# Weight refills of a routed expert layer: four parts in four slots, and an early product moved past the refill tables

## The chip, the cores and the metric

The kernel runs on one core of a Trainium2 chip. The metric is the device time of one execution in microseconds (us); before the change the median of 3 runs is 1395.26 us (1395.2 to 1396.17). The engines are TensorE (PE in the rows; PEld is its weight load), VectorE (DVE), ScalarE (ACT), GpSimd (POOL) and SyncE (SP), which here issues nearly all transfers.

## The reference

Three layers in a row on 4608 tokens of width 512: attention within chunks of 64 (8 heads), a dense layer of width 2048, and a routed layer with 8 experts of width 1024. Only the last matters here:

```python
expert_idx = np.argmax(x @ w_gate, axis=1)
for e in range(E):
    mask = expert_idx == e
    h = np.maximum(x[mask] @ w1[e], 0.0)
    out[mask] = gate_w[mask, None] * (h @ w2[e])
```

Each token goes through one expert, and how many go to which is known only once all of them have been gated.

## The kernel before

**Slots.** While the dense layer runs, each token's row is written to a table in DRAM (`xs`), sorted by expert. The expert stage then works through it in slots: one slot is a block of 128 tokens of one expert. Blocks of one expert stand next to each other. A static loop (line 948) covers `TS` = 39 slots, numbered from 0; an optional tail covers more.

**Weights.** An expert's weights are four parts of 2 MB: parts 0 and 1 are the two halves of `w1`, parts 2 and 3 those of `w2`. They lie split in two float32r pieces in DRAM (`wsp`), and in `ring[0]` to `ring[3]` on chip. Every ring tile has two halves, so that one expert can be in work while the next one's part is loaded. Which half a slot reads is a run-time value (`rt` row 0, read by TensorE's sequencer in `m1`, line 683).

**What a slot does.** `load(t)` (line 637): SP reads the slot's place and issues five transfers, the input rows in four and two columns (`gi`) in a fifth; the input has three buffers. `tx(t)` transposes the input (VectorE) and splits it (ScalarE, GpSimd). `m1(t, 0)` and `m1(t, 1)` are 12 products of 128x512 each, with parts 0 and 1; evictions go to ScalarE for the first and to VectorE for the second. `th(t, f)` transposes and splits the result. `m2(t, 0)` and `m2(t, 1)` are 12 products each with parts 2 and 3; then the result is scaled and scattered to the output. All products are recorded on line 677.

**Refills.** `refill(t, c)` (line 856) is called for every slot t from 4 on and every part c, and issues one transfer from SP (line 861) with a condition that is read from `rt[3 + c, t]`. Where the condition is 0, nothing is moved, but SP goes through the instruction and its waits all the same. The transfer writes the half that slot t doesn't read. Since halves are run-time values, the bookkeeping sees a write of the whole part; line 869 declares that the readers in slots t and t+1 don't depend on it, so the first products that wait for `refill(t, c)` are those of slot t+2 with part c. In the other direction the refill waits for the last product of slot t-1 with that part.

**Order.** The order of work is written by hand: every engine runs its instructions in the order of the program. Up to slot 5 it is the list `START` (line 886). From then on the loop's iteration t records tx(t+2), m1(t+1, 0), refill(t, 0), m1(t+1, 1), refill(t, 1), th(t+1), m2(t, 0), refill(t-1, 2), m2(t, 1), refill(t-1, 3), load(t+4). So on SP four refills and one load follow each other in each iteration, in order.

**Tables.** The rows of `rt` are made on VectorE on one partition, for 50 slots at once. `table_refill` (line 840) makes the conditions: `mt` is the number of blocks of the slot's expert less 2, `rr` the place of the slot in its expert (0, 1, ...), `has` says that there is a next expert to load. The expert of the first slots needs no refill: the first two experts are loaded ahead. Before the change part c is loaded in the slot in which `rr` is min(mt, c // 2), that is parts 0 and 1 in the expert's first slot and parts 2 and 3 in its second (all four in the first where it has two blocks).

Of the kernel before, what the change touches and what calls it, by code (L numbers as in the profile page):

```python
# [12 lines left out]
ALU = mybir.AluOpType  # L13
# [29 lines left out]
def tile_attention_moe(ctx, tc, q, k, v, w_in, w_out, alpha, w_gate, w1, w2, out):  # L43
# [13 lines left out]
    T = NTILE + 2 * (E - 1)  # L57
# [525 lines left out]
    V = nc.vector  # L583
# [133 lines left out]
    def tbl(shape, name, dt=F32):  # L717
        tb[name] = P2["tb"].tile(shape, dt, name=name)
        return tb[name]

    def bc(x, a, b, p=128):
        return x.unsqueeze(1).to_broadcast([p, b - a, E])
# [90 lines left out]
    def slot_sum(dst, vals):  # L813
        w = tb["w"][o1]
        V.tensor_tensor(out=w, in0=tb["oh"][o1], in1=vals, op=ALU.mult)
        V.tensor_reduce(out=dst, in_=w, axis=AX.X, op=ALU.add)
# [23 lines left out]
    def table_refill():  # L840
        q_ = tb["ordt"]
        mt, rr, cm, has = (tbl([1, T], x) for x in ("mt", "rr", "cm", "has"))
        mo = tbl([1, 1], "mo")
        V.tensor_reduce(out=mo, in_=tb["pos8"][o1, 1], axis=AX.X, op=ALU.max)
        V.tensor_scalar(out=has, in0=q_, scalar1=mo[:, 0:1], scalar2=None, op0=ALU.is_lt)
        V.scalar_tensor_tensor(out=has, in0=q_, scalar=0.5, in1=has, op0=ALU.is_gt, op1=ALU.mult)
        V.scalar_tensor_tensor(out=has, in0=tio[o1], scalar=tb["S"][o1, 0:1], in1=has, op0=ALU.is_lt, op1=ALU.mult)
        slot_sum(mt, bc(tb["m"][o1], 0, T, 1))
        slot_sum(rr, tb["d"][o1])
        V.tensor_copy(out=rt[:, 7, T:T + 1], in_=tb["S"][o1])  # L850
        V.tensor_scalar(out=mt, in0=mt, scalar1=-2.0, scalar2=None, op0=ALU.add)
        for c in range(4):
            V.scalar_tensor_tensor(out=cm, in0=mt, scalar=float(c // 2), in1=rr, op0=ALU.min, op1=ALU.is_equal)
            V.tensor_tensor(out=rt[:, 3 + c, 0:T], in0=cm, in1=has, op=ALU.mult)

    def refill(t, c):
# [23 lines left out]
    for t in range(3):  # L880
# [11 lines left out]
        (load_early, 1, 3), (table_own, 0, 8), (table_base, 0, 8), (th, 2, 0), (table_own, 8, T), (th, 2, 1), (load, 4),  # L892
        (tx, 4), (m1, 3, 0), (table_order,), (m2, 1, 0), (m1, 3, 1), (m2, 1, 1), (load, 5), (m2, 2, 0), (th, 3, 0),
        (tx, 5), (m2, 2, 1), (table_next,), (load, 6), (th, 3, 1), (m1, 4, 0), (m1, 4, 1), (tx, 6), (th, 4, 0),
        (table_base, 8, T), (m2, 3, 0), (th, 4, 1), (load, 7), (table_refill,), (m1, 5, 0), (refill, 4, 0), (load, 8),
        (m2, 3, 1), (th, 5, 0), (m1, 5, 1), (refill, 4, 1), (m2, 4, 0), (th, 5, 1), (m2, 4, 1),
    )
    FIRST = 5

# [123 lines left out]
```

## Time and profile before

| what | before |
|---|---|
| median of 3 runs | 1395.26 us |
| the profiled execution, its own time | 1394.91 us |
| its span, first to last instruction | 1393.1 us |
| PE busy | 1333.0 us (96%) |
| PEld busy | 1153.9 us (83%) |
| DVE busy | 1028.5 us (74%) |
| ACT busy | 817.2 us (59%) |
| POOL busy | 744.2 us (53%) |
| granted TensorE clock, mean | 0.99 |

The page of the profile cuts the span into 40 slices and gives each engine's busy share in tenths; PE stands at 9 from the fifth slice to the 37th, with one 8. The share says little about single waits: a few us in a slice of 35 don't show. They are found in the view of waits (who waited for whom) and in the timeline, which has one line for a run of like instructions on an engine: start, duration, engine, line, operation, names, count, and in brackets the idle time before it and what ended it. A line that begins with `SPq` is an issue by SyncE; its duration is that of the issue, not of the transfer. The expert stage runs from 933 us to the end.

### The profile page before, as it was taken

What the parts mean: (1) busy time and instruction counts of PE and PEld (TensorE: products, weight loads), DVE (VectorE), ACT (ScalarE), POOL (GpSimd) and SP (SyncE); (2) the same over time, 40 slices, a digit from 0 to 9 for tenths busy, and PEclk for the clock granted to TensorE, in tenths of its full rate; (3) what the DMA queues carried; (4) which work ended last, traced back from release to release, by engine and by line L of the source; (5) the groups of instructions that cost most, each with busy time, mean ns of one, the idle gap of its engine ahead of it and who ended that gap; (6) DMA issues with size and microseconds to landing.
All of it is one profiled execution on the core that took longest, in us unless ns stands there. A gap on an engine that the chain in (4) does not pass through costs nothing. (4 is left out here: it accounts for less than half of the span.)

```text
span 1393.1 us, 31133 instructions
## 1 busy us (share of the span) xinstructions
PE 1333.0 (96%) x9515; PEld 1153.9 (83%) x9515; DVE 1028.5 (74%) x2526; ACT 817.2 (59%) x2281; POOL 744.2 (53%) x754
## 2 busy tenths in 40 slices
PE   7788999999999999999999999999899999989997
PEld 6667888998999999999999998887688888868775
DVE  7996688788788878878887886668966655555553
ACT  4554565656656565656656564349565566646554
POOL 4553457666665766666666664334444444424443
PEclk9999999999999999999999999999999999999999
DMA  6545445556556665655566551293124416865543
GB/s 231 197 151 183 146 161 199 187 189 207 197 171 200 196 204 182 202 183 194 179 216 197 168 184 45 62 413 112 43 61 167 167 54 224 340 243 209 173 167 147
DMA packets 107306, 249.16 MB, mean 179 GB/s; under 512 B 15552, under 2 KB 36544, under 8 KB 103040
## 3 DMA queue, kind: packets, MB, share of 16 engines
q1 hardware_dynamic: 101136, 227.37, 48.1%
q0 software_dynamic: 6000, 19.70, 3.7%
q8 instruction: 84, 1.38, 0.4%
q14 instruction: 86, 0.70, 0.2%
HBM read 401.39 MB, written 88.91 MB: 352 GB/s over the span
## 5 line engine op out<-in xcount | busy, mean ns | idle before, releaser
L328 PEld LDWEIGHTS h<-xt,ring 128*128 128x128 f32 x3456 | 455.8, 192 | 41.7 <-DVE xt L315 4.0
L328 PE MATMUL h<-xt,ring 128*128 128x256 f32 x3456 | 465.8, 285 | 14.3 <-DVE xt L315 3.5
L380 PE MATMUL y<-ring,g 128*128 128x512 f32 x1728 | 457.5, 400 | 5.4 <-POOL g L358 3.0
L380 PEld LDWEIGHTS y<-ring,g 128*128 128x128 f32 x1728 | 307.5, 190 | 62.9 <-POOL g L358 4.7
L358 POOL TENSOR_TENSOR g<-r,g 128x256 fp32r<-128x256 f32 x281 | 249.3, 890 | 137.3 <-ACT g L354 121.4
L404 DVE CUSTOM_DVE_ANT_0 junk<-row,wgb 128x512 bf16<-128x512 f32 x288 | 267.5, 929 | 7.8 <-ACT row L392 3.6
L468 POOL TENSOR_TENSOR sp<-eraw,sp 128x512 fp32r<-128x512 f32 x128 | 181.8, 1421 | 132.4 <-ACT sp L467 117.0
L695 DVE TENSOR_SCALAR hx<-h 32x128 f32<-32x128 f32 x576 | 165.3, 287 | 108.5 <-PE h L677 101.1
L677 PE MATMUL h<-ring,xT 128*128 (+1 forms) x936 | 227.7, 398 | 11.3 <-DMA ring<-wsp 9.9
L665 POOL TENSOR_TENSOR hT<-z,hT 128x512 fp32r<-128x512 f32 x78 | 100.6, 1308 | 238.5 <-ACT hT L664 238.5
L677 PE MATMUL y<-ring,hT 128*128 (+1 forms) x936 | 221.5, 391 | 5.0 <-POOL hT L665 3.0
L677 PEld LDWEIGHTS h<-ring,xT 128*128 128x128 f32 x936 | 176.5, 189 | 55.2 <-issue 6.7
L677 PEld LDWEIGHTS y<-ring,hT 128*128 128x128 f32 x936 | 175.2, 188 | 45.5 <-POOL hT L665 4.7
L354 ACT ACTIVATE g<-r 128x256 fp32r<-128x256 f32 x288 | 119.5, 415 | 151.7 <-DVE r L350 109.6
L344 ACT ACTIVATE r<-h 128x256 f32<-128x256 f32 x288 | 109.9, 381 | 159.5 <-POOL g L358 74.5
L693 ACT ACTIVATE hx<-h 32x128 f32<-32x128 f32 x672 | 179.6, 267 | 12.7 <-PE h L677 5.2
L664 ACT ACTIVATE hT<-z 128x512 fp32r<-128x512 f32 x78 | 48.0, 632 | 131.4 <-DVE z L662 127.2
L257 ACT ACTIVATE px<-s 32x256 f32<-32x256 f32 x240 | 89.7, 374 | 3.8 <-DVE s L246 0.9
L467 ACT ACTIVATE sp<-eraw 128x512 fp32r<-128x512 f32 x128 | 81.1, 633 | 1.0
L662 DVE STREAM_TRANSPOSE z<-xg 128x512 f32<-128x512 f32 x39 | 27.6, 708 | 47.3 <-POOL hT L665 47.2
L665 POOL TENSOR_TENSOR xT<-z,xT 128x512 fp32r<-128x512 f32 x39 | 52.2, 1337 | 16.7 <-ACT xT L664 16.2
L269 POOL TENSOR_TENSOR px<-px,sr 128x512 f32<-128x512 f32 x30 | 34.1, 1136 | 39.8 <-DVE sr L268 39.8
(734 smaller groups left out, 1192.9 us busy)
## 6 DMA issues: line engine op xcount, KB each, us to landing
ring<-wsp SPq DMA_DIRECT2D x148, 2048.0 KB
wsp<-sp SPq DMA_DIRECT2D x128, 512.0 KB
eraw<-in_w SPq DMA_DIRECT2D x128, 256.0 KB
xg<-xs SPq DMA_DIRECT2D x156, 64.0 KB
vt<-in_v SPq DMA_DIRECT2D x18, 512.0 KB
qt<-in_q SPq DMA_DIRECT2D x17, 512.0 KB
kt<-in_k SPq DMA_DIRECT2D x17, 512.0 KB
iraw<-in_w_in SPq DMA_DIRECT2D x16, 512.0 KB
```

The source lines that it names most:

```text
L257: nc.scalar.activation(out=p[J:J + 32, t], in_=s[I:I + 32, e], func=ACTF.Exp, scale=scale)
L328: nc.tensor.matmul(out=h, lhsT=w[:, wl, a, 128 * mi:128 * mi + 128], rhs=x[:, xl, a], start=(n == 0), stop=(n == 11),)
L344: nc.scalar.activation(out=r, in_=h, func=ACTF.Relu)
L354: nc.scalar.activation(out=gs[j, m][:, 0], in_=rs[j, m][0], func=ACTF.Copy)
L358: eng.tensor_tensor(out=g[:, 1], in0=r, in1=g[:, 0].bitcast(F32), op=ALU.subtract)
L380: nc.tensor.matmul(out=ys[j][t], lhsT=g[:, gl, 128 * t:128 * t + 128], rhs=w[:, wl, mi], start=(m == 0 and n == 0), stop=(m == MF - 1 and ...
L404: nc.vector.tensor_tensor_reduce(out=junk, in0=r[:, 0:512], in1=wgb[e // 2][:, e % 2], scale=1.0, scalar=0.0, op0=ALU.mult, op1=ALU.add, a ...
L468: eng.tensor_tensor(out=dst[:, 1], in0=raw, in1=dst[:, 0].bitcast(F32), op=ALU.subtract)
L665: nc.gpsimd.tensor_tensor(out=dst[:, 1], in0=z, in1=dst[:, 0].bitcast(F32), op=ALU.subtract)
L677: ins.append(nc.tensor.matmul(out=out, lhsT=lhs[:, xl, a], rhs=w[:, rows_, wl, a], start=(first and a == 0 and n == 0), stop=(last and a = ...
L693: nc.scalar.activation(out=dst, in_=src, func=ACTF.Relu)
L695: V.tensor_scalar(out=dst, in0=src, scalar1=0.0, scalar2=None, op0=ALU.max)
```

## The change

Two edits. In `table_refill`, parts 1 and 2 get their own condition: with `far` = 1 where the slot's expert has five or more blocks (`mt` >= 3) and 0 elsewhere, part 1 is loaded where `rr` is min(mt, 0) + far, part 2 where it is min(mt, 1) + far; part 0 where it is min(mt, 0) as before, and part 3 where it is min(mt, 3). So an expert with five or more blocks loads parts 0, 1, 2 and 3 of the next in its slots 0, 1, 2 and 3; one with four blocks in 0, 0, 1 and 2; one with three in 0, 0, 1, 1 and one with two in its first slot, both as before. In `START`, `m1(5, 0)` moves in front of `table_refill`, and `load(8)` moves from behind `refill(4, 0)` to behind `refill(4, 1)`.

```diff
         V.tensor_scalar(out=mt, in0=mt, scalar1=-2.0, scalar2=None, op0=ALU.add)
+        far = tbl([1, T], "far")
+        V.tensor_scalar(out=far, in0=mt, scalar1=3.0, scalar2=None, op0=ALU.is_ge)
         for c in range(4):
-            V.scalar_tensor_tensor(out=cm, in0=mt, scalar=float(c // 2), in1=rr, op0=ALU.min, op1=ALU.is_equal)
+            if c in (1, 2):
+                V.scalar_tensor_tensor(out=cm, in0=mt, scalar=float(c - 1), in1=far, op0=ALU.min, op1=ALU.add)
+                V.tensor_tensor(out=cm, in0=cm, in1=rr, op=ALU.is_equal)
+            else:
+                V.scalar_tensor_tensor(out=cm, in0=mt, scalar=float(c), in1=rr, op0=ALU.min, op1=ALU.is_equal)
             V.tensor_tensor(out=rt[:, 3 + c, 0:T], in0=cm, in1=has, op=ALU.mult)
...
-        (table_base, 8, T), (m2, 3, 0), (th, 4, 1), (load, 7), (table_refill,), (m1, 5, 0), (refill, 4, 0), (load, 8),
-        (m2, 3, 1), (th, 5, 0), (m1, 5, 1), (refill, 4, 1), (m2, 4, 0), (th, 5, 1), (m2, 4, 1),
+        (table_base, 8, T), (m2, 3, 0), (th, 4, 1), (load, 7), (m1, 5, 0), (table_refill,), (refill, 4, 0),
+        (m2, 3, 1), (th, 5, 0), (m1, 5, 1), (refill, 4, 1), (load, 8), (m2, 4, 0), (th, 5, 1), (m2, 4, 1),
```

## Rows read from the trace of the kernel before

**Rows 1.** Waits of TensorE from 930 us: total us, times, longest.
```profile
PE h L677 <- DMA ring<-wsp: 9.9, 5, 2.6
...
PE h L677 <- DVE cm L853: 1.5, 1, 1.5
```

**Rows 2.** Timeline of TensorE: start, us, engine, line, operation, names, count, [idle before].
```profile
983.56 2.96 PE L677 MATMUL h<-ring,xT 128*128 x12
...
1001.11 3.04 PE L677 MATMUL h<-ring,xT 128*128 x12 [1.48 <-DVE cm L853]
1005.71 3.03 PE L677 MATMUL h<-ring,xT 128*128 x12 [1.57 <-DMA ring<-wsp]
...
1014.05 5.76 PE L677 MATMUL h<-ring,xT 128*128 x24
...
1213.25 5.76 PE L677 MATMUL h<-ring,xT 128*128 x24
...
1227.07 3.04 PE L677 MATMUL h<-ring,xT 128*128 x12 [2.60 <-DMA ring<-wsp]
1232.60 4.45 PE L677 MATMUL h<-ring,xT 128*128 x12 [2.48 <-DMA ring<-wsp]
...
1242.35 5.76 PE L677 MATMUL h<-ring,xT 128*128 x24
...
1291.07 3.04 PE L677 MATMUL h<-ring,xT 128*128 x12 [1.49 <-DMA ring<-wsp]
...
1310.48 5.76 PE L677 MATMUL h<-ring,xT 128*128 x24
...
1348.36 3.03 PE L677 MATMUL h<-ring,xT 128*128 x12 [1.72 <-DMA ring<-wsp]
...
1356.69 5.76 PE L677 MATMUL h<-ring,xT 128*128 x24
```

**Rows 3.** A stretch: its us, PE busy (products), granted clock, DMA share, GB/s.
```profile
1232.40:1235.60 3.20, 3.00 (x7) 0.50 0.03 12
```

**Rows 4.** Timeline of SP, refill(4, 0) and refill(4, 1), no data moved.
```profile
1000.87 0.12 SPq L861 DMA_DIRECT2D ring<-wsp  x1
...
1005.49 0.10 SPq L861 DMA_DIRECT2D ring<-wsp  x1
```

**Rows 5.** Timeline of VectorE, `table_refill`: first and last of four flags.
```profile
999.61 0.20 DVE L854 TENSOR_TENSOR rt<-cm,has 1x50 int32<-1x50 f32 x1
...
1001.01 0.20 DVE L854 TENSOR_TENSOR rt<-cm,has 1x50 int32<-1x50 f32 x1
```

**Rows 6.** Timeline of SP: refill groups, single refills, a load (xg), refill(36, 3).
```profile
1112.64 3.55 SPq L861 DMA_DIRECT2D ring<-wsp  x4
...
1121.76 3.55 SPq L861 DMA_DIRECT2D ring<-wsp  x4
...
1206.77 0.37 SPq L861 DMA_DIRECT2D ring<-wsp  x1
1208.23 0.35 SPq L861 DMA_DIRECT2D ring<-wsp  x1
...
1214.17 0.37 SPq L861 DMA_DIRECT2D ring<-wsp  x1
1215.62 0.35 SPq L861 DMA_DIRECT2D ring<-wsp  x1
...
1328.37 1.90 SPq L645 DMA_DIRECT2D xg<-xs  x4
...
1370.23 0.09 SPq L861 DMA_DIRECT2D ring<-wsp  x1
```

**Rows 7.** SP's waits for ring DMAs: 1060 to 1100, 1236 to 1300, from 1000.
```profile
SPq L861 <- DMA ring<-wsp: 8.9, 3, 5.1
...
SPq L861 <- DMA ring<-wsp: 8.1, 2, 4.7
...
SPq L861 <- DMA ring<-wsp: 48.4, 14, 5.1
```

**Rows 8.** A stretch: its us, five engines' busy time, granted clock, DMA share, GB/s.
```profile
905.00:906.00 1.00, 1.00 (x7) 0.87 (x6) 0.36 (x1) 0.61 (x2) 0.00 (x0) 1.00 1.03 442
```

## The prediction

> **What bounds the kernel now.** I read the waits of TensorE first, for the expert stage only (from 930 us). Only two lines matter for this change: 9.9 us in five waits for the weight refills (`ring<-wsp`), and 1.5 us put down to a table instruction of line 853 [rows 1]. Then the timeline of TensorE, to see where these lie and what each really costs. A slot is 24 products of the first layer and 24 of the second. Where nothing waits, the start-to-start of two slots is 11.07 us: from slot 7 (1014.05) to slot 25 (1213.25) are 18 slots in 199.20 us with no idle time [rows 2]. So TensorE sets the time of this stage, and everything above 11.07 us per slot is loss:
> - slot 6 to slot 7: 1001.11 to 1014.05 is 12.94, a loss of 1.87. Its second half waits for a ring DMA.
> - slot 25 to slot 27: 1213.25 to 1242.35 is 29.10 against 22.13, a loss of 6.97. Both halves of slot 26 wait (2.60 and 2.48 idle), and then the second half takes 4.45 us where 12 products else take about 3.0 [rows 2]. In that stretch the granted clock reads 0.50, the 1.2 GHz level [rows 3].
> - slot 27 to slot 37: 1242.35 to 1356.69 is 114.34 against 110.67, a loss of 3.67, at the second halves of slots 31 (1.49 idle) and 36 (1.72 idle) [rows 2].
>
> Together 12.51 us, 0.9% of the run. This is all that the change can reach in TensorE's waits.
>
> **Which refills are meant.** SP issues a refill for every slot and part, with a condition. An issue whose condition fails takes about 0.1 us, a real one 0.35 [rows 6]. Working the reference's routing through for the drawn inputs gives 3, 2, 9, 5, 10, 1, 5 and 4 blocks of 128 tokens, the expert with one block last: 39 slots, just the static loop. In the order of the kernel: 10 (slots 0 to 9), 9 (10 to 18), 3 (19 to 21), 2 (22, 23), 5 (24 to 28), 5 (29 to 33), 4 (34 to 37), 1 (38). The real issues at slots 22 and 24 in the timeline of SP fit [rows 6]. Now parts 0 and 1 leave in the first slot of an expert and parts 2 and 3 in the second. After the change the experts with 9, 5 and 5 blocks send one part in each of four slots; the one with 4 keeps parts 0 and 1 together and sends part 3 a slot after part 2; those with 3 and 2 stay as they are.
>
> **The spread of the parts, term by term.** A product of slot t+2 waits for the refill issued for slot t, needed or not: the half is a run-time value, and only slots t and t+1 are declared free of it.
>
> Slot 26 waits for parts 0 and 1 of slot 24. Four parts leave at 1206.77, 1208.23, 1214.17 and 1215.62 [rows 6], and the last lets slot 26 go at 1232.60 [rows 2]: 25.8 us for four, 6.5 each. The change moves the fourth to the next slot. Three take 3 x 6.5 = 19.4 us and would land at 1226.1 if they left when they do now. Without its wait, and 1.6 us earlier for the start of the loop (below), slot 26 begins at 1213.25 + 11.07 - 1.6 = 1222.7. That is 3.4 us too early, so it also matters whether SP comes sooner. I think it does. SP works in order, and a group of four conditional issues and five loads takes it 9.12 us if nothing holds it (1112.64 to 1121.76 [rows 6]), against 11.07 for TensorE, so SP catches up 1.95 us a slot when it is late. It is late: it was held until the tables were ready, and then for 8.9 us behind the pairs of slots 10 and 11 [rows 7]. Those pairs are now single parts. One part takes 6.5 us by the sum above, less than a group of SP, so the hold goes. SP then reaches slot 22 about 8.9 us sooner, the three parts land at 1217.2, and slot 26 finds them there with 5.5 us to spare. The wait of its second half goes with part 1, which now has a slot of its own, and so does the stretch at half clock, which came right behind the two waits. **6.97 us**.
>
> Slot 31: parts 0 and 1 of slot 29 are parted, and SP's further hold of 8.1 us in this stretch [rows 7] goes too. Slot 36 still waits for a pair (its expert has four blocks). There the gain is SP's alone: the wait ends if SP issues 1.7 us sooner in relation to TensorE. It fetches the input of slot 37 at 1328.37, when slot 33 has been in work since 1310.48 [rows 2, 6], though its buffer is free once the input of slot 34 is transposed, at the start of slot 33. That lag of nearly 18 us is made of the holds that go (8.9 + 8.1). **3.67 us**.
>
> **The start of the loop.** In front of slot 6 the order on SP is: refill(4, 0), input of slot 8, refill(4, 1). Both refills are without data here, yet slot 6 waits for them: its halves start at 1001.11 and 1005.71 [rows 2], 0.24 and 0.22 us after the two issues at 1000.87 and 1005.49 [rows 4]. With the load behind, refill(4, 1) follows refill(4, 0) after about 1.15 us (four issues in 3.55 [rows 6]), at 1002.3, long before the second half of slot 6 wants it (1001.11 + 2.8 = 1003.9). This gives back 1.87. The load of slot 8 leaves 1.4 us later; TensorE needs it at slot 8, some 22 us on, so I cost it at nothing.
>
> The tables get three more VectorE operations on 50 elements: `far`, and one more each for parts 1 and 2. One of this size takes 0.20 us, 0.235 with the step to the next: from 999.61 to 1001.01 are six steps [rows 5]. One of the three, `far`, lies in front of the flag of part 0, for which refill(4, 0) and so slot 6 wait: 0.24 us lost. The other two delay the transposes of slot 5 behind them by 0.47 us; these have to be ready for the second layer of slot 5, which now begins earlier. I bound that between 0 and 0.5 and take the middle. So 1.87 - 0.24 - 0.23 = **1.4 us**.
>
> The first product of slot 5 in front of the tables: it starts at 983.56 without idle time [rows 2], 16 us before the flags are written from 999.61 on [rows 5]. It doesn't wait for them now, its evictions are on ScalarE, and no table instruction is there. On no engine does the order change: **0**. Were there a hidden wait, it would have shown there, so I exclude gain and loss.
>
> **Terms that could go the other way.** Parts 2 and 3 of the five-block experts leave one and two slots later, with slots 28 and 29 as first readers in the kernel's bookkeeping: by the same two-slot rule over 20 us for a part that takes 7. Part 3 of the expert with four blocks moves from slot 35 to 36, and slot 38, the last, waits for it. Its present place on SP, without data, is at 1370.23 [rows 6]. If SP is on time it leaves some 20 us earlier.
>
> **Sum.** 6.97 + 3.67 + 1.4 = 12.0 us. The profiled execution is 1394.91 us with a span of 1393.1, 0.35 under the median of 1395.26. I take the gain from the median: 1395.26 - 12.0 = **1383.2 us**.
>
> **A rule set against this.** The sum above uses 6.5 us per part, from the row. The Trainium skill (DMA: Bandwidth & Descriptors, "Anatomy of one DMA") prices a transfer at 2.0 us plus its bytes over 436 GB/s, fitted on another issue path; as an estimate, three parts of 2.1 MB back to back would take 16.4 us, not 19.4, and slot 26 would wait 0.5 us rather than 3.4 even with SP as late as now.
>
> **Rivals.**
> 1. *SP stays late*, because something else holds it. Then slot 26 still waits 3.4 us: 1383.2 + 3.4 = 1386.6. For it: the experts with three and two blocks still send pairs at slots 19 to 23. If the wait at slot 36 stays as well, 1.9 more: 1388.5. Against: the 8.9 us of holds at slots 10 to 13 belong to parts that are spread.
> 2. *A remaining wait brings the low clock*: 4.45 - 3.0 = 1.4 us more on top of rival 1, 1388.0. In the trace only the two waits in a row at slot 26 are followed by 0.50 [rows 3]; at slots 31 and 36 the loss of 3.67 is little more than the 3.21 of idle time. [...]
> 3. *The last part comes late.* If SP lags at the end as now, part 3 leaves at 1370.2 and lands 7 us on, at 1377; slot 38's second half, 12 us earlier than now, wants it at about 1370. 7 us back: 1390.
> 4. *The waits go and the next engine is late at the same places*, or the flags don't spread the parts at all: only the start of the loop is left, 1393.8. Against: 18 slots in a row ran without a wait of any kind [rows 2], and experts with five and nine blocks exist.
> 5. *Slower.* A single part lands as late as a pair does, say because one transfer can't fill the DMA engines. The largest hold of SP was 5.1 us [rows 7]; if every slot from 24 to 37 held it so, SP's slot is 14.2 us instead of 11.07, and over 14 slots it falls 43 us behind, of which its lead covers about 20. TensorE loses 23: 1406. It decides when a hold passes 11.07 - 9.12 = 1.95 us a slot. Against: with one part and one input load in flight the DMA share is 1.03 at 442 GB/s [rows 8].
>
> **Chances.** Forecast 0.62; rival 1 0.15; rival 2 0.05; one term alone missing (1384.6 to 1387) 0.05; rival 3 0.03; rival 4 0.06; rival 5 0.04. Range 1381.8 to 1388.0: it holds the forecast with the loop's start at its full worth, rival 1 and rival 2, and leaves out the rest. A measurement of this kernel tells about 0.2% (2.8 us) from no change; only rival 4 lies within it. Faster 0.90, same 0.06, slower 0.04.
>
> **What will show it.** Right: no wait of TensorE for ring DMAs after slot 6, start-to-start 11.07 through slots 25 to 27, no low clock there; issues of 0.35 us alone in slots 10 to 13, 24 to 27 and 29 to 32; far less than 48.4 us of SP waiting for ring DMAs [rows 7]; slot 6 still waiting about 1.7 us for the tables. Wrong: a ring wait at slot 26 (rival 1) or at slot 38 (rival 3), or SP held in every slot (rival 5).

## The result, and the profile after

The changed kernel takes 1383.68 us (median of 3 runs, 1382.6 to 1384.84) against 1395.26 before: a ratio of 0.9915, 95% interval 0.9898 to 0.9932, that is 11.6 us less. The forecast was 1383.2 us, in a range of 1381.8 to 1388.0. Run again beside the last experiment, its ratio was 0.9903 (0.9887 to 0.992).

TensorE's waits from 930 us on, answering to [rows 1] (total us, times, longest):

```profile
PE h L677 <- DVE cm L857: 1.6, 1, 1.6
PE h L677 <- DMA ring<-wsp: 0.3, 1, 0.3
```

The waits for weight refills went from 9.9 us in five to 0.3 in one. The one for the tables (line 853 before, 857 now) went from 1.5 to 1.6. The timeline of TensorE at the places of [rows 2]:

```profile
975.56 5.76 PE L677 MATMUL h<-ring,xT 128*128 x24
...
1000.19 5.84 PE L677 MATMUL h<-ring,xT 128*128 x24 [1.60 <-DVE cm L857]
...
1011.58 5.76 PE L677 MATMUL h<-ring,xT 128*128 x24
...
1210.76 5.76 PE L677 MATMUL h<-ring,xT 128*128 x24
...
1222.28 5.83 PE L677 MATMUL h<-ring,xT 128*128 x24 [0.29 <-DMA ring<-wsp]
...
1344.08 5.76 PE L677 MATMUL h<-ring,xT 128*128 x24
```

These are the starts of slots 4, 6, 7, 25, 26 and 37. From slot 7 to slot 37 the loop takes 332.50 us (1011.58 to 1344.08), where 30 slots at 11.07 are 332.0; before it was 342.64 (1014.05 to 1356.69 in [rows 2]). **10.1 us** of the gain lie there. Slot 6 to slot 7 went from 12.94 to 11.39, **1.55 us**. Together 11.7; the two spans differ by 11.2 (1393.1 and 1381.9). The rest is outside of the change: slot 4 began 0.35 us later, slots 4 to 6 came out 1.3 us shorter and the end behind slot 37 1.4 us longer, and the third experiment below shows that the last two move as much between two executions of the same program.

The granted clock in the stretch around slot 26 (columns as in [rows 3]) is full, where it was at half for a while before:

```profile
1222.00:1228.00 6.00, 5.72 (x25) 1.00 0.29 51
```

The timeline of SP: the group of slot 10 and the last transfer of the load behind it, the groups of slots 11 and 15, part 2 of slot 22, parts 0 and 1 of slot 24, part 0 of slot 34, part 3 of slot 36:

```profile
1054.06 4.20 SPq L867 DMA_DIRECT2D ring<-wsp  x4
...
1062.45 0.36 SPq L648 DMA_DIRECT2D gi<-xs  x1
1065.00 3.83 SPq L867 DMA_DIRECT2D ring<-wsp  x4
...
1105.62 5.04 SPq L867 DMA_DIRECT2D ring<-wsp  x4
...
1200.85 0.37 SPq L867 DMA_DIRECT2D ring<-wsp  x1
...
1208.61 0.37 SPq L867 DMA_DIRECT2D ring<-wsp  x1
...
1210.07 0.10 SPq L867 DMA_DIRECT2D ring<-wsp  x1
...
1318.69 0.37 SPq L867 DMA_DIRECT2D ring<-wsp  x1
...
1352.47 0.36 SPq L867 DMA_DIRECT2D ring<-wsp  x1
```

Part 1 of slot 24 is now empty (0.10 us where it was 0.35 in [rows 6]). SP's waits for ring DMAs from 1000 us on, against 48.4 us in [rows 7]:

```profile
SPq L867 <- DMA ring<-wsp: 25.8, 14, 4.3
```

This is the refills' own line. On line 648, the fifth transfer of an input load, SP's waits for ring DMAs rose in the same stretch from 8.3 us to 11.6, six waits in either.

### The profile page after: what moved, and what is told of

The parts are those of the page before. It is cut to its first block, busy times and chain, and to the rows that moved or that the text cites. A ratio compares the mean times of both kernels' runs of the same rounds, so it can differ in the third digit from the quotient of the medians.

```text
span 1381.9 us, 31135 instructions
## 1 busy us (share of the span) xinstructions
PE 1333.5 (96%) x9515; PEld 1156.5 (84%) x9515; DVE 1029.6 (75%) x2529; ACT 818.3 (59%) x2281; POOL 745.3 (54%) x754
## 5 line engine op out<-in xcount | busy, mean ns | idle before, releaser
L344 ACT ACTIVATE r<-h 128x256 f32<-128x256 f32 x288 | 110.1, 382 | 158.6 <-POOL g L358 74.5
```

What stands on the lines that cost most here:

```text
L344: nc.scalar.activation(out=r, in_=h, func=ACTF.Relu)
```

## The experiments

Two measures stand for the two places: slots 7 to 37 (30 x 11.07 = 332.0 if nothing waits), and slot 6 to 7 or 4 to 7, both from the timeline of TensorE of one profile. The ratio is over all the runs of a kernel, to the kernel before run beside it; for SP early it is that of the first round, and the other two gave 0.9946 each. A single profile is weak where refills are waited for: SP early, one program, gave loops 5.1 us apart. The four loops with hardly a ring wait (changed twice, conditions alone, SP early and spread) lie between 332.00 and 332.51.

| kernel | ratio, 95% interval | slot 6 to 7 | slots 7 to 37 |
|---|---|---|---|
| before | | 12.94 | 342.64 |
| changed | 0.9915 (0.9898 to 0.9932) | 11.39 | 332.50 |
| changed, again | 0.9903 (0.9887 to 0.992) | 11.37 | 332.01 |
| conditions alone | 0.9917 (0.9904 to 0.993) | 12.87 | 332.51 |
| load of slot 8 alone | 0.9994 (0.9984 to 1.0003) | 11.13 | 344.46 |
| product of slot 5 alone | 1.0009 (1.0 to 1.0018) | 12.96 | 342.30 |
| spread for nine blocks alone | 0.9979 (0.9967 to 0.9991) | 11.63 | 342.62 |
| spread for five blocks alone | 0.9963 (0.9949 to 0.9978) | 11.62 | 338.48 |
| SP early, no spread (three profiles) | 0.9945 (0.9925 to 0.9965) | 12.50 to 12.53 | 342.56, 337.43, 338.12 |
| SP early and spread | 0.991 (0.9897 to 0.9924) | 13.10 | 332.00 |
| start drawn up anew | 0.9903 (0.9887 to 0.992) | 11.44 | 335.25 |

### The conditions alone

The new conditions in `table_refill`, `START` as before.

> The new conditions alone, the order of the start as before. Stage measure: from the start of slot 7's first product to slot 37's, 342.64 us before and 332.50 after the change (30 slots at 11.07 are 332.0); slot 6 to slot 7 12.94 before, 11.39 after. Theory (the spread carries the loop's gain, the moved load the start's): slots 7 to 37 in 332.0 to 334, with SP about as early as after the change; slot 6 to 7 still near 12.7, with the second half of slot 6 waiting some 1.3 to 1.6 us for refill(4, 1); total 1384.5 to 1386.5, gain 9 to 11. Rival (the start's edit makes SP early and that is what counts in the loop): slots 7 to 37 stay above 338.

Slot 6, its second half, and slots 7 and 37 in its timeline of TensorE:

```profile
1001.70 3.03 PE L677 MATMUL h<-ring,xT 128*128 x12 [1.58 <-DVE cm L857]
1006.23 3.03 PE L677 MATMUL h<-ring,xT 128*128 x12 [1.50 <-DMA ring<-wsp]
...
1014.57 5.76 PE L677 MATMUL h<-ring,xT 128*128 x24
...
1347.08 5.76 PE L677 MATMUL h<-ring,xT 128*128 x24
```

As the theory had it: the loop's gain is all here (332.51), and slot 6's second half still waits 1.50 us for refill(4, 1). The rival, that the start's edit carries the loop, falls. In the ratios the start's edit can't be seen: 0.9917 here, 0.9915 and 0.9903 with it. Its 1.5 us are read from the profiles alone (slot 6 to 7 in 12.87 here, 11.39 and 11.37 with it).

### The load of slot 8 alone

```diff
-        (table_base, 8, T), (m2, 3, 0), (th, 4, 1), (load, 7), (table_refill,), (m1, 5, 0), (refill, 4, 0), (load, 8),
-        (m2, 3, 1), (th, 5, 0), (m1, 5, 1), (refill, 4, 1), (m2, 4, 0), (th, 5, 1), (m2, 4, 1),
+        (table_base, 8, T), (m2, 3, 0), (th, 4, 1), (load, 7), (table_refill,), (m1, 5, 0), (refill, 4, 0),
+        (m2, 3, 1), (th, 5, 0), (m1, 5, 1), (refill, 4, 1), (load, 8), (m2, 4, 0), (th, 5, 1), (m2, 4, 1),
```

> Only the input load of slot 8 behind refill(4, 1), old conditions. Theory: slot 6 to 7 falls from 12.94 to about 11.1 to 11.4 and nothing else does; slots 7 to 37 stay at 341 to 344 with ring waits at slots 26, 31 and 36; total 1393 to 1394.5, gain 1 to 2. Rival (SP's order at the start sets its lateness in the loop): ring waits at 26, 31 and 36 shrink by a third or more, total under 1391.

Its timeline of TensorE, slots 6, 7, the waits at 26, 31 and 36, and slot 37:

```profile
1001.44 5.84 PE L677 MATMUL h<-ring,xT 128*128 x24 [1.50 <-DVE cm L853]
...
1012.57 5.76 PE L677 MATMUL h<-ring,xT 128*128 x24
...
1226.89 4.58 PE L677 MATMUL h<-ring,xT 128*128 x12 [2.97 <-DMA ring<-wsp]
...
1290.56 3.04 PE L677 MATMUL h<-ring,xT 128*128 x12 [2.56 <-DMA ring<-wsp]
...
1348.69 3.04 PE L677 MATMUL h<-ring,xT 128*128 x12 [2.56 <-DMA ring<-wsp]
...
1357.03 5.76 PE L677 MATMUL h<-ring,xT 128*128 x24
```

Half a miss. Slot 6 to 7 gained 1.81 us as expected, but the total didn't move: slots 7 to 37 took 344.46, 1.82 more than before. TensorE arrived earlier at slots 26, 31 and 36, the refills landed within 0.5 us of when they did before (slot 37 starts at 1357.03 against 1356.69), and the gain was waited away: the median, 1395.35, lies above the 1393 to 1394.5 expected. The edit gives its 1.5 us only where the ring waits are gone too, as in the profiles of the changed kernel.

### The product of slot 5 alone

```diff
-        (table_base, 8, T), (m2, 3, 0), (th, 4, 1), (load, 7), (table_refill,), (m1, 5, 0), (refill, 4, 0), (load, 8),
+        (table_base, 8, T), (m2, 3, 0), (th, 4, 1), (load, 7), (m1, 5, 0), (table_refill,), (refill, 4, 0), (load, 8),
```

> Only the first product of slot 5 in front of the refill tables. Listed by engine, instructions and waits are those of the kernel before, one by one, so this is the kernel before run once more. Theory: 1395.3 within 1.5 us, slots 7 to 37 in 342 to 343. What it tells besides: how much the stretch ahead of slot 6 (38.84 us from slot 4's first product to slot 7's before, 36.02 after the change) and the end behind slot 37's start (36.41 before, 37.82 after) move from one execution to the next. If both stay within 0.3 us, the change itself moved them; if they move by 1 us or more, they are no part of it.

Its timeline of TensorE, slots 4, 7, two waits at 26 and 31, and slot 37:

```profile
975.66 5.76 PE L677 MATMUL h<-ring,xT 128*128 x24
...
1013.05 5.76 PE L677 MATMUL h<-ring,xT 128*128 x24
...
1226.34 4.59 PE L677 MATMUL h<-ring,xT 128*128 x12 [2.87 <-DMA ring<-wsp]
...
1290.14 4.21 PE L677 MATMUL h<-ring,xT 128*128 x12 [2.67 <-DMA ring<-wsp]
...
1355.35 5.76 PE L677 MATMUL h<-ring,xT 128*128 x24
```

This part of the change does nothing: on every engine instructions and waits stay the same, in the same order. The profile is therefore a second look at the kernel before, and shows what one execution alone can't. Slot 4 to slot 7 is 37.39 here and 38.84 in the profile of before (975.21 to 1014.05), the end behind slot 37 37.8 (span 1393.1) and 36.4: both move by 1.4 us with nothing changed. The ring waits sit elsewhere too, 12 products in 4.59 and 4.21 us at slots 26 and 31 and no wait at slot 36, yet slots 7 to 37 add up to 342.30, almost the same.

### The spread for nine blocks alone, and for five alone

In the first `far` is 1 only for the nine-block expert; in the second only for those with five. Elsewhere the conditions of before hold. The diff, against the changed kernel, is that for nine; for five the comparison is `is_equal` to 3.0. Both have one VectorE operation more in the tables (`far2`).

```diff
...
-        V.tensor_scalar(out=far, in0=mt, scalar1=3.0, scalar2=None, op0=ALU.is_ge)
+        V.tensor_scalar(out=far, in0=mt, scalar1=7.0, scalar2=None, op0=ALU.is_ge)
+        V.tensor_scalar(out=far2, in0=far, scalar1=2.0, scalar2=None, op0=ALU.mult)
         for c in range(4):
-            if c in (1, 2):
-                V.scalar_tensor_tensor(out=cm, in0=mt, scalar=float(c - 1), in1=far, op0=ALU.min, op1=ALU.add)
+            if c:
+                V.scalar_tensor_tensor(
+                    out=cm, in0=mt, scalar=float(c // 2), in1=far2 if c == 3 else far, op0=ALU.min, op1=ALU.add,
+                )
...
```

> The spread for the expert with nine blocks alone (slots 10 to 18); those with five and four blocks send pairs as before; start as after the change. Theory (two causes at slot 26: SP's lateness, and the fourth part): SP reaches slot 24 about 5.6 us sooner than before, as after the change, but four parts of 6.5 to 7 us each are ahead of slot 26's second half again: it waits 2 to 4.5 us there, less at its first half (0 to 1); waits at slots 31 and 36 fall under 1 us or vanish, since SP is earlier; total 1386.5 to 1389.5. Rival A (lateness alone): no ring wait at 26, total as after the change, 1383 to 1385. Rival B (the fourth part alone): waits at 26, 31 and 36 as before, total 1393.

Timeline of TensorE, slots 7 and 25, both halves of slot 26, the second half of slot 36, slot 37; then part 0 of slot 24 in the timeline of SP:

```profile
1012.03 5.76 PE L677 MATMUL h<-ring,xT 128*128 x24
...
1211.23 5.76 PE L677 MATMUL h<-ring,xT 128*128 x24
...
1222.77 3.03 PE L677 MATMUL h<-ring,xT 128*128 x12 [0.31 <-DMA ring<-wsp]
1228.42 4.41 PE L677 MATMUL h<-ring,xT 128*128 x12 [2.62 <-DMA ring<-wsp]
...
1344.76 4.58 PE L677 MATMUL h<-ring,xT 128*128 x12 [2.47 <-DMA ring<-wsp]
...
1354.65 5.76 PE L677 MATMUL h<-ring,xT 128*128 x24
```

```profile
1209.05 0.37 SPq L870 DMA_DIRECT2D ring<-wsp  x1
```

SP came to slot 24 at 1209.05, as early as in the changed kernel, and slot 26's first half waited 0.31 us, its second 2.62: both as expected. The waits at slots 31 and 36 should have fallen under 1 us and didn't (slot 31: 1.18 idle in its second half; slot 36: 2.47 idle, then 12 products in 4.58 us). The loop gained nothing, 342.62, and the median, 1393.18, is not the 1386.5 to 1389.5 expected but that of rival B (the fourth part alone, 1393). Against rival B stands that slot 26's first half waited only 0.31 us, where it was 2.60 before.

> The spread for the two experts with five blocks alone; those with nine and four blocks send pairs as before (part 3 of the one with four too); start as after the change. Theory: SP is held at slots 10 to 13 as before and comes to slot 24 at about 1214 (1208.6 after the change); the three parts ahead of slot 26 land 13.6 us later, as after the change, at about 1227.8, where slot 26 would begin at some 1222: its first half waits 4 to 6 us, its second none; no wait at slot 31; at slot 36 none or under 1.5. Slots 7 to 37 in 336.5 to 339; total 1387 to 1390. Rival A (the nine-block expert's spread does nothing): 7 to 37 at 332.5, total as after the change. Rival B (all of the gain is the nine-block expert's; the run with that alone had 342.6): 7 to 37 above 341.

Timeline of TensorE, slots 7, 26 and 37; then part 0 of slot 24 in the timeline of SP:

```profile
1012.03 5.80 PE L677 MATMUL h<-ring,xT 128*128 x24
...
1227.18 7.36 PE L677 MATMUL h<-ring,xT 128*128 x24 [3.91 <-DMA ring<-wsp]
...
1350.51 5.76 PE L677 MATMUL h<-ring,xT 128*128 x24
```

```profile
1213.60 0.37 SPq L870 DMA_DIRECT2D ring<-wsp  x1
```

Nearly as expected: SP at slot 24 at 1213.60, no wait at slots 31 and 36, and slots 7 to 37 in 338.48; slot 26's first half waits 3.91 us, just under the 4 to 6. The two spreads don't add: alone they are worth 0.0 and 4.2 us in the loop, by one profile each, together 10.1.

### SP early, without and with the spread

The refills of slots 4 to 9 are left out. They carry no data for these inputs; with a first expert of four blocks the second expert's refills would be among them. First with the old conditions:

```diff
     def refill(t, c):
+        if t < 10:
+            return
```

> Old conditions, start as after the change, and the refills of slots 4 to 9 left out of the program: for these inputs they move nothing, so the output is the reference's here, but inputs with a short first expert would need them. SP then waits for no table ahead of slot 10 and spares six groups of about 4.6 us. Theory (both causes): slot 6 no longer waits for the tables (slot 4 to slot 7 near 34.5 to 36); SP is on time at slot 10, is held by the pairs of slots 10 and 11 as before, and slot 26's second half still waits 1 to 4 us, slots 31 and 36 1.5 to 4; slots 7 to 37 at 337 to 342; total 1388 to 1392. Rival (SP's lateness alone makes the ring waits): 7 to 37 at 332 to 334, total 1381 to 1384, without spreading anything.

Its executions lay apart (1385.05 to 1393.28), so it was run twice more for further profiles:

> The old conditions without the refills of slots 4 to 9 once more (they move nothing for these inputs). Its first executions fell into two groups, four at 1385.0 to 1387.9 and two at 1393.1 to 1393.3, and the profile is of the second, with slots 7 to 37 in 342.56. Theory (with SP early, the pairs are at the edge: the waits at slots 31 and 36 come or don't come, as the first hold falls): an execution of the first group has 7 to 37 in 334 to 337, with the wait at slot 26 and little behind it. Rival (the groups differ ahead of slot 7 or behind slot 37): 7 to 37 at 341 to 343 in either group.

> The same kernel again, for a further profile. Theory: as in the run before; 7 to 37 in either 334 to 337 or 341 to 343, and the total goes with it. Rival: totals differ with 7 to 37 the same.

In the first profile slot 26's second half waits 2.14 us; in the third slot 26 waits for nothing. The third's timeline of TensorE, slots 7, 25 and 27, the second halves of 31 and 36, and slot 37; then parts 0 of slots 24 and 34 in its timeline of SP:

```profile
1010.43 5.76 PE L677 MATMUL h<-ring,xT 128*128 x24
...
1209.62 5.76 PE L677 MATMUL h<-ring,xT 128*128 x24
...
1231.76 5.76 PE L677 MATMUL h<-ring,xT 128*128 x24
...
1280.19 3.03 PE L677 MATMUL h<-ring,xT 128*128 x12 [1.20 <-DMA ring<-wsp]
...
1338.70 4.57 PE L677 MATMUL h<-ring,xT 128*128 x12 [2.95 <-DMA ring<-wsp]
...
1348.55 5.76 PE L677 MATMUL h<-ring,xT 128*128 x24
```

```profile
1202.94 0.37 SPq L863 DMA_DIRECT2D ring<-wsp  x1
...
1323.25 0.38 SPq L863 DMA_DIRECT2D ring<-wsp  x1
```

With SP early alone (in the third profile it waited 33.8 us for VectorE to free input buffers) the loss of slots 7 to 37 stays at 10.6 us in the first profile and falls to 5.4 and 6.1 in the other two. In those two slot 26's loss of 6.97 is gone although all four parts are still ahead of it: part 0 of slot 24 left 6.4 and 6.7 us ahead of the start of slot 25. It left 3.9 us ahead in the first profile and 2.2 in the run for nine blocks alone, where slot 26's second half waits 2.14 and 2.62. So enough lead does at slot 26 what the spread does there; at the lead that the changed kernel has, 2.2 us, the fourth part must go too. The waits at 31 and 36 stay in all three and cost 5.4 to 6.6 us together, more than the 3.67 before. The rival, lateness alone, falls there: it wanted 332 to 334. Of the later expectation, that the total goes with slots 7 to 37 holds for the 5 us between the groups. But 334 to 337 was too low, and the places were the wrong way round: a wait at slot 26 and little behind it was expected.

Why the later waits stay is in SP's pace. From part 0 of slot 24 to part 0 of slot 34 SP takes 1323.25 - 1202.94 = 120.3 us, 12.0 per slot, and TensorE needs 11.07; in the changed kernel it is 1318.69 - 1208.61 = 110.1, 11.0 per slot. The other profiles agree: 118.3 to 121.9 in all seven with pairs in the five-block experts, 108.1 to 110.6 in all six without. With such pairs SP falls some 8 to 11 us behind TensorE's 110.7 in ten slots, and a lead is used up.

Then with the new conditions:

> The changed kernel with the refills of slots 4 to 9 left out of the program (they move nothing for these inputs; others may need them). Theory: the last 0.3 us wait at slot 26 goes, since SP comes sooner, and slots 7 to 37 take 332.0; slot 6 doesn't wait for the tables: slot 4 to slot 7 falls from 36.0 by 1.5 to 2; total 2 to 2.5 us under the changed kernel, 1381 to 1382.5. Rival (VectorE's chain of slot 5 holds slot 6 and 7 anyway): slot 4 to slot 7 stays within 0.5 us of 36.

Timeline of TensorE, slot 6, the second half of slot 5's second layer, slot 7:

```profile
998.78 5.76 PE L677 MATMUL h<-ring,xT 128*128 x24
...
1008.11 0.73 PE L677 MATMUL y<-ring,hT 128*128 x2 [0.82 <-ACT hT L664]
...
1011.88 5.76 PE L677 MATMUL h<-ring,xT 128*128 x24
```

Slots 7 to 37 take 332.00, with no ring wait at all, as expected, and the median, 1382.34, is inside the 1381 to 1382.5. At the start the rival won: slot 6 no longer waits for the tables, but slot 5's second layer then waits for its transpose, and slot 4 to slot 7 is 35.95 against 36.02 (37.39 when the changed kernel was run again); nor is the ratio better than the changed kernel's. The wait for the tables is worth nothing while VectorE's chain of tables and transposes behind it is as long.

### The start drawn up anew

The changed kernel with that chain shortened, and the load of slot 8 ahead of the tables on SP:

```diff
-        (load_early, 1, 3), (table_own, 0, 8), (table_base, 0, 8), (th, 2, 0), (table_own, 8, T), (th, 2, 1), (load, 4),
+        (load_early, 1, 3), (table_own, 0, 9), (table_base, 0, 9), (th, 2, 0), (table_own, 9, T), (th, 2, 1), (load, 4),
...
-        (table_base, 8, T), (m2, 3, 0), (th, 4, 1), (load, 7), (m1, 5, 0), (table_refill,), (refill, 4, 0),
-        (m2, 3, 1), (th, 5, 0), (m1, 5, 1), (refill, 4, 1), (load, 8), (m2, 4, 0), (th, 5, 1), (m2, 4, 1),
+        (m2, 3, 0), (th, 4, 1), (load, 7), (load, 8), (m1, 5, 0), (table_refill,), (refill, 4, 0),
+        (m2, 3, 1), (th, 5, 0), (m1, 5, 1), (refill, 4, 1), (m2, 4, 0), (th, 5, 1), (m2, 4, 1), (tx, 7), (table_base, 9, T),
...
-            if two: tx(t + 2)
+            if two and t > FIRST: tx(t + 2)
```

> The changed kernel with the start drawn up anew: the long table of row places (4.2 us of VectorE) goes from in front of slot 4's second transpose to behind the transposes of slots 5 and 7, and the input load of slot 8 in front of the wait for the refill tables on SP. Theory (VectorE's chain of tables and transposes holds slots 4 to 6, as the run without the refills of slots 4 to 9 showed, where slot 5's second layer waited for its transpose at 1006.68): slot 4 to slot 7 falls from 36.0 to 33.3 to 34.3, SP comes some 4 us sooner and the 0.3 us wait at slot 26 goes; slots 7 to 37 in 332.0; 1.8 to 3 us under the changed kernel. Rival (another engine of that stretch is late next, or the loads of slots 8 and 9 come late for TensorE): slot 4 to slot 7 stays above 35.5, no gain over the changed kernel.

and beside it the changed kernel again:

> The changed kernel once more, beside the next one on the same chip. Theory: ratio to the kernel before 0.9905 to 0.993; slots 7 to 37 in 332.0 to 333.2 (332.50 in its first profile), slot 6 to 7 in 11.2 to 11.7.

Timeline of TensorE of the new start, slots 4 and 7, slot 6's second layer, slot 26:

```profile
972.28 5.76 PE L677 MATMUL h<-ring,xT 128*128 x24
...
1007.37 5.76 PE L677 MATMUL h<-ring,xT 128*128 x24
1013.82 0.73 PE L677 MATMUL y<-ring,hT 128*128 x2 [0.69 <-ACT hT L664]
...
1220.81 5.83 PE L677 MATMUL h<-ring,xT 128*128 x24 [1.15 <-DMA ring<-wsp]
```

Slot 4 to slot 7 fell to 35.09, 2.3 us under the changed kernel beside it (1010.06 less 972.67, 37.39), though not to the 33.3 to 34.3 expected. It was all given back: slot 6's second layer now waits for the transposes behind the moved table, and slot 26, which TensorE reaches earlier, waits 1.15 us for its refill. The ratios are the same, 0.9903 both (medians 1380.97 and 1381.61). No version here beats the changed kernel clearly.

## Why the prediction was right, point by point

- **What could be gained.** 12.51 us of loss read from start-to-start times; 11.7 were recovered, 0.45 is left at slot 26 and 0.32 at slot 6. Reading start-to-start and not idle time was needed: the idle time alone was 9.9. That the total came within 0.5 us is in part luck: two stretches outside of the change moved by -1.3 and +1.4 us.
- **The spread.** 10.64 forecast, 10.1 measured, and the run with the conditions alone shows that it is theirs. The mechanism at slot 26 (SP's lateness and the fourth part) was the right one. With SP late and the fourth part gone it waits 3.9 us, where rival 1 had 3.4; with SP as early as the change brings it and the fourth part kept, 2.6. Both must go at that lead; at 6.4 us or more SP's lead alone was enough.
- **Terms that were mis-sized there.** SP was to reach slot 22 8.9 us sooner with 5.5 us to spare; it was 5.6 sooner at slot 24 (1214.17 to 1208.61), and nothing was to spare (0.29 us of waiting). The step that failed is "the hold goes": a single part still holds SP, and needs longer than I gave it. The one of slot 10 left at 1054.06, and the ninth issue from there (`gi`, line 648) was held for it and went only at 1062.45, 8.4 us later, where I had 6.5. The one of slot 11 left at 1066.17, and the ninth issue from there, at 1075.51, was held too: it looks as if each issue waits for the one eight before it to land, which is read from such places and not shown otherwise. From slot 11 to 15 SP took 10.2 us a group (1065.00 to 1105.62 in four), not 9.12. Three parts took 21.4 (1200.85 to 1222.28), not 19.4. So the parts left 3.0 us later than forecast and took 2.0 longer, and slot 26 wanted them 0.9 earlier: that uses up the 5.5 us. Rival 1 had just begun, and that it cost no more than 0.45 us is luck.
- **Slot 36.** That SP's gain alone ends its wait was right, but the reason was thinner than the truth: not a lag that is removed once, but a pace. Pairs in the five-block experts keep SP slower than TensorE (12.0 against 11.07 us a slot), which the run for nine blocks alone showed and my expectation for it had missed.
- **The start.** 1.4 forecast for the table and the load together, 1.55 less 0.12 for the longer wait for the tables (1.48 to 1.60) measured. (In the working for slot 26 the prediction has 1.6 for this term; the 0.2 decide nothing.) But rival 4's price, the start alone at 1393.8, was wrong: alone it gives nothing, since the next ring wait takes it back.
- **The product of slot 5.** 0, and the program shows it.
- **The last part.** It leaves at 1352.47, 17.8 us before its empty place of before [rows 6]; no wait at slot 38.
- **The low clock.** It went with the waits. In the profiles with ring waits it came behind waits of 2.1 to 3.9 us, eleven times in all (granted clock 0.50 to 0.77 over the products behind them), and didn't behind three of 2.56 to 2.60 nor behind any of 1.72 or less. It came behind single waits too and at all three slots, so rival 2's reading, that only two waits in a row bring it, was that of one execution; its 1.4 us could come at any of the three. The Trainium skill (TensorE: Matmul & The Clock Gate, "HAM oscillation") describes a kernel in which waits for data of some 3 to 5 us brought the low clock each time. Here ten of the eleven waits were shorter, 2.1 to 3.0 us, and waits of such a length didn't bring it each time.
- **The slower rival.** A single part lands well before a pair did: before, the pair of slot 10 left from 1055.01 on and held SP until 1068.74, 13.7 us, against 8.4. A single part's hold of SP averages 10.16 - 9.12 = 1.0 us a slot against the 1.95 from which it would have decided. That margin is smaller than I had thought.

## What to carry to other kernels

Where several waits on one slow resource follow each other, moving the consumer forward can gain nothing, and removing one cause gains less than its share (here 0 to 5 of 10 us): compare the resource's pace per step with the consumer's, and look for the edit that brings it under. Spreading transfers helps here not by moving fewer bytes but by keeping an in-order issuing engine from being held behind a pair. A gain at the start counts only if no later wait is tied to something that didn't move.

## What the runs showed of the hardware

An issue whose condition is false still costs SyncE about 1.15 us with its register loads, and the product that waits for it starts 0.2 us after it: 116 of the 140 refills carry nothing, and with four of them an SP step that moves no weights spends 4.4 of its 9.12 us on them (1112.64 to 1117.02 in the timeline of SP before). One 2 MB part, alone in flight but for an input load and a result, let its waiter go 8.4 us after its issue; three behind each other took 21.4 and four 25.8, so a further one added 5.8 to 6.5. By the fit of the Trainium skill (DMA: Bandwidth & Descriptors, "Anatomy of one DMA"), made for another issue path, one part would take, as an estimate, 2.0 us plus 2.1 MB over 436 GB/s, 6.8 us; this trace has 1.6 more.
